# A long convolution on one core: products written over their spectrum, and a last sum of 32x32 tiles in place of transposes

## The chip, the core and the metric

The kernel runs on one core of a Trainium2 chip. The metric is the device time of one launch in microseconds, the median of several runs of the same program. The core has five engines with a queue of instructions each: PE (the 128x128 matrix unit, whose weight loads are listed apart as PEld), DVE (vector), ACT (scalar, activation functions), POOL (general purpose) and SP (which here only issues DMAs). An instruction that waits holds up all that stand behind it in the queue of its engine. Matmuls write to PSUM, four buffers of 128x1024 f32 named p in this stage; DVE or ACT carry a result from there to SBUF, which is called an evacuation below.

## The reference

Two kinds of layer alternate, twice each, over 2048 tokens of 512 channels. Layer A is a gated long convolution along the tokens, layer B an MLP of width 1376. The long convolution is given as an FFT of length 4096:

```python
def _A_ref(q, k, v, shift_k, ssm_k, ssm_D):
    ...
    for t in range(ks):                       # 4 taps along the tokens
        k_shift = k_shift + k_pad[:, t:t + S, :] * shift_k[:, ks - 1 - t][None, None, :]
    kv = k_shift * v
    ...
    y_f = kv_f * kf_f[None, :, :, :]          # spectra of kv and of the filter ssm_k
    y = irfft2(y_f) ...[:, 0, :S, :]
    y = y + kv * ssm_D[None, None, :]
    return q * y

def _B_ref(x, w1, b1, w2, b2):
    y = _layernorm(x, axis=-1)
    h = _gelu(jnp.einsum("bsd,df->bsf", y, w1) + b1)
    return jnp.einsum("bsf,fd->bsd", h, w2) + b2

x = A_q
x = x + _A_ref(_layernorm(x), A_k, A_v, A_shift_k, A_ssm_k, A_ssm_D)
x = x + _B_ref(_layernorm(x), B_w1, B_b1, B_w2, B_b2)
x = x + _A_ref(_layernorm(x), ...)
x = x + _B_ref(_layernorm(x), ...)
```

The convolved y does not depend on x, so it is the same in both layers A. Only the gate, layer norm of x times y, differs.

## The kernel before, in words

The kernel has a planned stage, in which y is computed once and the MLP's first pieces begin, and a dense loop behind it, in which PE runs the MLP's two matmuls back to back (mm1 at L735 with gelu on ACT, mm2 at L769), 4 blocks of 512 tokens in each of the two layers.

The planned stage splits the 512 channels into four chunks of 128 (cc = 0 to 3) and the transform of 2048 tokens into 32 by 64 points. Each step is a piece of work with a name, and a second piece with an e behind its name evacuates it:

- kT and kv (L439, L521): the short convolution of k on PE as matmuls with diagonal weights, for chunks 0 to 2; kvm multiplies by v (L527, DVE). Chunk 3 is done on POOL by kg0 to kg3, ka1 to ka3 (L453, L455, L460) and kgm, which multiplies by v (L464).
- U{cc}S{q}: first stage of the forward transform (L303). U{cc}T{j}: its 32-point pieces are transposed, on PE for chunks 0 to 2 (L335), by two DMA transposes for chunk 3 (L282); the result is ZX.
- kd, KS, K2 (L382, L390, L403): the spectrum of the filter, ZK. K2 are matmuls of 64 rows, two at a time in two groups of rows. The spectrum is needed a second time with the two halves of each complex pair exchanged between partitions; that is KSW, 64 KB further, made by eight copies of 512 KB from SBUF to SBUF by DMA, sa0 to sa3 and sb0 to sb3.
- X{cc}{j}: second stage of the forward transform, eight matmuls of 128 columns into a buffer xb (L551). T{cc}{j}: product with the filter, xb times ZK and KSW in one DVE instruction of 128x2048 into a buffer T (L566). V{cc}{j}: the first step of the inverse, sixteen matmuls whose weights are slices of T against a table Mt of 2 MB that holds the twiddle factors (L575).
- Z, TC, TD and so on: V's results are transposed again, by DMA (L622) or PE (L610). Y: the last step, matmuls of 512 columns with the table GPt (L642). Then for the first block of tokens the gate g (L669, L670), statistics h, p, b (L237, L249, L254), LT (L650, transposing the normed x for the MLP) and M (L698), the first mm1 with its gelu (L706). lx and ly are loads of q, 512 KB and 1536 KB, into x_t.

The order of the work is written out by hand in a string, ORDER. Each of its words names a piece, its engine (P, A, D, G for POOL, S for SP) and its buffers; `_Plan.write` issues the pieces word for word, so each engine's queue has its pieces in the order of the words. The semaphores are put in behind that, by what reads and writes the same range of memory: most of the data lies in one SBUF tile called arena, and the names above are places in it. The product reads both spectra with one access:

```python
kk = at(64 * K + 2 * (ka * D + c0), [[-32 * K, 2], [D, n], [1, CW]])     # KSW, and 64 KB below it ZK
...
eng.tensor_tensor(view(Tb[it["slot"]["T"]], [2, n, CW]), x2, kk, ALU.mult)
```

Of the kernel before, what the change touches and what calls it, by code (L numbers as in the profile page):

```python
# [18 lines left out]
lSK.S wm2.P2 bS.P2 wm0.P1 bSe.A dg0.D dg1.A dg2.A lk0.S lk1.S lh1.S kT0.P2 bSK.P1 bSKe.A kT0e.D kT1.P0 kT2.P3 lh113.S lb1.S lx0.S kT1e.D kT2e.A kT3.P1 wm1.P0 bB.P2 bBe.A lv0.S s00.A lv1.S kT3e.D kv10.P3 kvm10.D kv00.P1 U1S0.P30 kv01.P2 kvm00.D U1S1.P1 U0S0.P01 U1S0e.D lK01.S kg0.G kv11.P3 lK00.S kg1.G U0S0e.A kvm01.D U0S1.P0 s01.G U0S1e.A U0S3.P2 U1S1e.D kvm11.D U0S3e.A kv20.P1 kd0.P0 lK11.S lK10.S kvm20.D kd0e.A U1S3.P3 U0S2.P2 U1S3e.A U0S2e.D KS11.P0 KS11e.A KS01.P1 KS30.P3 KS01e.A lW.S KS00.P2 KS00e.A KS30e.D KS10.P0 KS31.P1 KS10e.D kv21.P3 kvm21.D KS31e.A kd4.P1 kd4e.A KS20.P0 KS21.P2 KS20e.A KS70.P1 KS21e.D KS51.P3 KS41.P0 KS70e.A KS51e.A KS60.P2 KS60e.A KS41e.D KS40.P1 KS61.P3 KS40e.D lX.S KS71.P0 KS50.P2 U1S2.P1 KS71e.D KS61e.A KS50e.A U1S2e.A U2S0.P32 U2S0e.D K25.P0 K25e.A K27.P2 K24.P1 K24e.A K23.P3 K21.P0 K21e.A K27e.D K26.P2 U2S1.P1 K26e.A K23e.D U2S1e.D K20.P3 K28.P0 K20e.A K22.P2 K22e.A K212.P1 K28e.D K215.P3 K215e.A lM.S K212e.D sa1.S sb1.S sa0.S K214.P0 K29.P2 K29e.A K213.P1 U0T0.P3 K214e.D K213e.A K210.P0 K210e.A sb0.S K211.P2 U0T1.P1 s02.D K211e.A U2S3.P0 U0T0e.D U2S3e.A U0T1e.D ka1.G kg2.G ka2.G kg3.G X00.P30 ka3.G kgm.G U3S0.P21 U3S0e.D U2S2.P1 X00e.A X01.P01 lH.S U2S2e.A U1T0.P3 U3S1.P2 T00.D0 U3S3.P1 X01e.A U1T1.P0 sb3.S U1T0e.D X10.P30 U3S1e.A U3S3e.A sa3.S X02.P22 T01.D1 X10e.A U2T0.P1 sb2.S U1T1e.D T10.D2 U3S2.P3 U2T0e.D X02e.A sa2.S X12.P01 V00.P2 U3S2e.A T02.D0 V10.P30 X12e.A X03.P10 V00e.A X03e.A V01.P0 V01e.A X20.P22 T12.D2 X20e.A U3T0.S V12.P1 X11.P01 X11e.A V10e.D lx.S V02.P3 U2T1.P2 T03.D1 X13.P00 T20.D2 V12e.A V02e.A T11.D0 V03.P1 U2T1e.D X13e.A V03e.A X30.P32 T13.D1 V11.P0 X30e.A V11e.D X23.P21 V13.P1 X23e.A U3T1.S V13e.A T30.D0 X22.P30 X22e.A T23.D1 V20.P01 X21.P22 ly.S X21e.A V20e.A V30.P12 X32.P31 T22.D2 T21.D0 X31.P20 V22.P0 X32e.A V21.P3 X31e.A V30e.D X33.P12 V22e.A Z01.S Z00.S X33e.A V23.P2 T32.D2 V23e.A T31.D0 V32.P0 V31.P1 T33b.D1 V33b.P2 T33a.D2 V31e.D Z11.S Z10.S V21e.A V32e.A V33a.P3 Z03.S V33ae.A TC0a.P0 TC0b.P1 Z13.S TC0ae.A TC0be.A w4.S V33be.D TD0b.P3 TD0a.P0 TD0ae.D TC3.P2 TD0be.A Y00.P0 Y01.P3 Y00e.A Y01e.A TC3e.D g00.D w1.S Z02.S TC1.P1 TC1e.A g01.D h00.D Y02.P2 Y32.P0 TC2.P3 Y02e.A h01.D Y32e.A Y10.P1 Y10e.A p00.G w3.S b00.D g02.D p01.G LT0.P2 LT0e.A Y12.P0 Y12e.A M0b.P1 M0be.A TC2e.A h02.D M0a.P2 b01.D LT1.P1 Y30.P0 LT1e.A p02.G b02.D LT2.P3 LG1.D LT2e.D M1a.P1 M0ae.A M1ae.A M1b.P2 M1be.A M2a.P3 M2ae.A M2b.P1 M2be.A M2c.P2 M2ce.A Y30e.A Z12.S w2.S Y20.P3 Y22.P1 Y20e.A Y22e.A  # L19
# [10 lines left out]
def _make_tables():  # L30
# [5 lines left out]
    G = np.zeros((128, 2, 128))  # L36
    for x in range(2):
        for bh in range(2):
            rows = 4 * a + 2 * bh + x
            F[rows, x, bh * 64:bh * 64 + 32] = np.cos(psi)  # L40
            F[rows, x, bh * 64 + 32:bh * 64 + 64] = np.sin(psi)
            for i, p in enumerate(rows):
                G[bh * 64:bh * 64 + 32, x, p] = np.cos(psi[i]) / 64
                G[bh * 64 + 32:bh * 64 + 64, x, p] = np.sin(psi[i]) / 64
# [3 lines left out]
    M = np.zeros((128, NA, 2, 128))  # L48
    for k in range(NA):
        phi = 2 * np.pi * (((k + 0.25) * b / 2048)[:, None] + np.outer(b, k2) / NB)  # L50
        c, s = np.cos(phi), np.sin(phi)
        for bh in range(2):
            cb, sb = c[bh * 32:bh * 32 + 32], s[bh * 32:bh * 32 + 32]
            r, i = bh * 64, bh * 64 + 32
            W[r:r + 32, k, 0:64] = cb
            W[r:r + 32, k, 64:128] = sb
            W[i:i + 32, k, 0:64] = -sb
            W[i:i + 32, k, 64:128] = cb
            for q, sign in ((0, 1.0), (64, -1.0)):
                M[q:q + 64, k, 0, r:r + 32] = sign * cb.T / 32  # L60
                M[q:q + 64, k, 0, i:i + 32] = -sign * sb.T / 32
                M[q:q + 64, k, 1, r:r + 32] = sb.T / 32
                M[q:q + 64, k, 1, i:i + 32] = cb.T / 32
# [5 lines left out]
    q = p % 32  # L69
    M = M[ri][:, :, :, p - q + 16 * (q // 4 % 2) + 4 * (q // 8) + q % 4]  # L70
    GP = G[32 * (p % 4) + p // 4]
# [3 lines left out]
    return tuple(_to_bf16_uint16(t) for t in (F, GP, W, np.roll(W, 64, axis=0), M))  # L75
# [29 lines left out]
def kernel(ctx: ExitStack, tc: tile.TileContext, A_q, A_k, A_v, A_shift_k, A_ssm_k, A_ssm_D,  # L105
                 B_x, B_w1, B_b1, B_w2, B_b2, out):
    nc = tc.nc
# [11 lines left out]
    NZT, NTB = 3, 3  # L119
# [5 lines left out]
    F_np, GP_np, W_np, X_np, M_np = _make_tables()  # L125
    F_h = nc.inline_tensor(F_np, name="tabF")
    GP_h = nc.inline_tensor(GP_np, name="tabGP")
    W_h = nc.inline_tensor(W_np, name="tabW")
    X_h = nc.inline_tensor(X_np, name="tabX")
    M_h = nc.inline_tensor(M_np, name="tabM")  # L130
# [20 lines left out]
    ZK = place("ZK", [P, NA, D], 0)  # L151
    ZX = place("ZX", [P, 2, NA, D // 2], 32 * K)
    Kd = place("Kd", [P, P, NB], 64 * K)
    Wx = place("Wx", [P, NA, P], 88 * K)
    Zk = place("Zk", [P, NA * 2, D // 2], 32 * K)
# [17 lines left out]
    GPt = const.tile([P, 2, P], BF16, name="GPt")  # L173
# [23 lines left out]
    def chunk(t, c):  # L197

        return t[:, c // 2, :, c % 2 * CW:c % 2 * CW + CW]


    ZTb = [big.tile([P, 8 * D], BF16, name=f"ZT{i}") for i in range(NZT)]
    xbb = [big.tile([P, 1024], BF16, name=f"xb{i}") for i in range(3)]
    Tb = [big.tile([P, 2048], BF16, name=f"T{i}") for i in range(NTB)]
# [15 lines left out]
    ZM = "XXPP"  # L220
# [629 lines left out]
```

## Time and profile before

| | us |
|---|---|
| median of 3 runs (lowest, highest) | 249.31 (249.17, 249.37) |
| profiled execution | 249.34 |
| its span, first to last instruction | 247.6 |
| planned stage, to the first mm2 (L769) | 101.4 |
| dense loop behind it | 146.2 |

The profile is one execution of the program. Its times are from the start of the span, and what lies outside the span (1.7 us) is launch and end. A row of a group gives line, engine, operation and tiles, then the count, the busy time in all and the mean in nanoseconds of one. Matmuls are pipelined, so the mean of one is longer than the distance from one to the next; in the chain of waits, which follows the work that ended last back to what released it, a row of matmuls gives their distance. In the timeline a row gives start and duration; an SP row gives the time in which the DMA was being issued, while the landing is in the list of DMA issues.

### The profile page before, as it was taken

The page shows a single profiled execution, that of the slowest core. Times are in us where ns is not written, and L with a number is a line of the kernel's source. Part 1 is how long each engine was busy: PE and PEld are TensorE (multiplying, and loading weights), DVE is VectorE, ACT ScalarE, POOL GpSimd, SP SyncE. Part 2 cuts the span into 40 slices and gives each one's busy share as a digit, 9 for nine tenths or more (in the row PEclk, how much of TensorE's full clock was granted, in tenths as well). Part 3 has the DMA queues.
Part 4 walks back from the last instruction along what each step waited for, and adds up shares of the span by engine and source line. Part 5 has one row for each costly group of instructions (what it writes and reads, how often), then busy time and mean ns, then how long its engine had stood idle before and what let it go on. Part 6 is the DMA issues. An engine that isn't in the chain of part 4 may idle for free.

```text
span 247.6 us, 4783 instructions
## 1 busy us (share of the span) xinstructions
PE 236.1 (95%) x1918; PEld 146.4 (59%) x1929; DVE 171.9 (69%) x315; ACT 145.1 (59%) x218; POOL 54.5 (22%) x50
## 2 busy tenths in 40 slices
PE   4999999899999999999999999999999999999994
PEld 2689877699998688444444444444444444444443
DVE  1467899999997988878889898956956961021022
ACT  5596899899999899707406506505605604704800
POOL 2789999400000221111101111011011010000000
PEclk9999999999999999999999999999999999999998
DMA  6999994946999990040601204013016016011011
GB/s 244 351 292 173 264 437 192 394 175 120 218 254 179 282 260 5 0 85 1 87 0 38 47 3 85 0 23 63 3 44 127 0 45 127 1 42 42 3 42 42
DMA packets 50816, 29.65 MB, mean 120 GB/s; under 512 B 44675, under 2 KB 48488, under 8 KB 49258
## 3 DMA queue, kind: packets, MB, share of 16 engines
q1 hardware_dynamic: 50642, 29.21, 45.7%
q8 instruction: 15, 0.25, 0.4%
q10 hardware_dynamic: 152, 0.14, 0.2%
q14 instruction: 7, 0.06, 0.1%
HBM read 16.23 MB, written 2.10 MB: 74 GB/s over the span
## 4 chain that ended last, share of the span: by engine, by line
PE 72%; DVE 9%; ACT 9%; DMA 5%; issue 2%; POOL 0%; ACTq 0%; DVEq 0%; POOLq 0%
PE po L769 31%; PE ph L735 27%; ACT arena L215 3%; DMA arena<-in_A_v_dram 3%; ACT xb L215 3%; PE p L521 3%; DVE arena L217 3%; ACT ZT L215 2%; DMA arena<-in_A_ssm_D_dram 2%; PE p L698 2%; PE p L303 2%; DVE arena L254 2%; PE p L403 1%; PE p L335 1%; PE p L575 1%
## 5 line engine op out<-in xcount | busy, mean ns | idle before, releaser
L737 ACT ACTIVATE arena<-ph,B 128x512 bf16<-128x512 f32 (+1 forms) x77 | 52.9, 687 | 78.6 <-PE ph L735 78.6
L769 PE MATMUL po<-arena 128*128 128x512 bf16 (+2 forms) x356 | 77.1, 372 | 0.4
L735 PE MATMUL ph<-arena 128*128 128x512 bf16 (+1 forms) x308 | 67.6, 379 | 0.0
L769 PEld LDWEIGHTS <-arena 128*128 128x128 bf16 (+1 forms) x363 | 35.4, 98 | 40.7
L774 DVE TENSOR_TENSOR arena<-po,arena 128x512 bf16<-128x512 f32 (+1 forms) x33 | 21.6, 672 | 44.6 <-PE po L769 44.5
L735 PEld LDWEIGHTS <-arena 128*128 128x128 bf16 (+1 forms) x308 | 30.8, 100 | 35.9
L215 ACT ACTIVATE arena<-p 128x1024 bf16<-128x1024 f32 (+7 forms) x44 | 40.6, 1005 | 3.6 <-PE p L383 1.2
L249 POOL TENSOR_TENSOR lrsm<-lrsm,mhalf 128x4 f32<-128x4 f32 (+2 forms) x10 | 9.1, 910 | 92.3 <-DVE lrsm L243 89.5
L237 DVE BATCH_NORM_STATS2 lstm<-arena 128x6 f32<-128x512 bf16 x32 | 20.0, 681 | 0.2
L215 ACT ACTIVATE ZT<-p 128x1024 bf16<-128x1024 f32 (+1 forms) x18 | 17.9, 1040 | 1.9 <-PE p L303 1.7
L566 DVE TENSOR_TENSOR T<-xb,arena 128x2048 bf16<-128x2048 bf16 (+1 forms) x17 | 18.9, 1153 | 0.0
L254 DVE TENSOR_SCALAR arena<-arena,lmvg,lrsg 128x512 bf16<-128x512 bf16 x32 | 12.9, 465 | 7.3 <-POOL lrsg L249 7.3
L249 POOL TENSOR_TENSOR lrsg<-lrsg,mhalf 128x4 f32<-128x4 f32 x8 | 8.1, 1012 | 44.6 <-DVE lrsg L246 44.6
L237 DVE BATCH_NORM_STATS2 lstg<-arena 128x6 f32<-128x512 bf16 x28 | 17.2, 677 | 0.0
L575 PE MATMUL p<-arena,T 128*128 128x128 bf16 x256 | 16.2, 219 | 0.6 <-ACT ZT L215 0.3
L215 ACT ACTIVATE xb<-p 128x1024 bf16<-128x1024 f32 x16 | 16.3, 1059 | 0.6 <-PE p L551 0.6
L217 DVE COPY arena<-p 128x2048 bf16<-128x2048 bf16 (+3 forms) x12 | 12.3, 1031 | 5.1 <-PE p L439 3.3
L575 PEld LDWEIGHTS <-T 128*128 128x128 bf16 x256 | 14.8, 98 | 1.1 <-issue 0.7
L453 POOL TENSOR_TENSOR T<-arena,SK 128x2048 bf16<-128x2048 bf16 (+3 forms) x4 | 15.0, 3760 | 1.3 <-ACT SK L215 1.1
L254 DVE TENSOR_SCALAR arena<-arena,lmvm,lrsm 128x512 bf16<-128x512 bf16 x32 | 11.5, 416 | 2.8 <-POOL lrsm L249 2.8
L217 DVE CAST arena<-p 128x1024 bf16<-128x1024 f32 x11 | 12.9, 1217 | 0.3
L217 DVE CAST ZT<-p 128x1024 bf16<-128x1024 f32 (+1 forms) x11 | 12.8, 1170 | 0.4 <-ACT arena L215 0.2
(80 smaller groups left out, 249.5 us busy)
## 6 DMA issues: line engine op xcount, KB each, us to landing
arena<-arena SPq DMA_DIRECT2D x8, 512.0 KB, 5.6
arena<-in_A_k_dram SPq DMA_DIRECT2D x2, 1024.0 KB, 6.2
arena<-in_A_v_dram SPq DMA_DIRECT2D x2, 1024.0 KB
arena<-in_A_ssm_k_dram SPq DMA_DIRECT2D x4, 512.0 KB, 12.1
arena<-tabM SPq DMA_DIRECT2D x1, 2048.0 KB
out_dram<-arena SPq DMA_DIRECT2D x15, 128.0 KB, 1.7
arena<-in_A_q_dram SPq DMA_DIRECT2D x1, 1536.0 KB, 6.8
arena<-in_B_w_dram SPq DMA_DIRECT2D x1, 1376.0 KB, 6.7
```

The source lines that it names most:

```text
L215: nc.scalar.activation(dst, src, AF.Copy)
L217: nc.vector.tensor_copy(dst, src)
L237: nc.vector.bn_stats(self.st[:, i, 0, :], x_t[:, GT * g + i, :] if src is None else src[:, i, :])
L249: nc.gpsimd.tensor_tensor(self.rs[:, a:b], self.rs[:, a:b], mhalf[:, a:b], ALU.pow)
L254: nc.vector.tensor_scalar(out=dst[:, i, :], in0=xs, scalar1=self.mv[:, i, 0:1], scalar2=self.rs[:, i:i + 1], op0=ALU.subtract, op1=ALU.mult)
L453: nc.gpsimd.tensor_tensor(m[:, t:NT, :], kn[:, 0:NT - t, c3], sk(t, NT - t), ALU.mult)
L566: eng.tensor_tensor(view(Tb[it["slot"]["T"]], [2, n, CW]), x2, kk, ALU.mult)
L575: nc.tensor.matmul(o[:, i, :], T[:, r, i, :], Mt[:, ka + i, 1 - r, :], start=r == 0, stop=r == 1)
L735: nc.tensor.matmul(o.rearrange("p (i t) -> p i t", t=P), W1t[:, ct, ft * P:ft * P + m], lt[:, a:b, ct, :], start=ct == 0, stop=ct == CT - 1)
L737: nc.scalar.activation(hT[0:m, ft, a * P:b * P], o, AF.Gelu_apprx_tanh, bias=B1[0:m, ft:ft + 1])
L769: nc.tensor.matmul(po[:, a:b], hT[0:m, ft, i * P:(i + 1) * P], W2t[0:m, ft, a:b], start=ft == 0, stop=ft == FT - 1)
L774: nc.vector.tensor_tensor(xs, po[:, a:b], xs, ALU.add)
```

## The change

- The filter's spectrum is made in two halves, chunks 1 and 3 first, then 0 and 2. K2 has 256 matmuls of 128 columns in place of 128 of 256. The eight copies sX are now one pair for each chunk (they were one pair for each quarter of the frequencies), and each waits for all K2 of its half.
- T writes its product over what it has read: over ZK and KSW themselves, with the same access of two steps 64 KB apart. The T buffers are gone; xb has five buffers in place of three.
- V is sixteen matmuls whose weights are slices of that product with a stride of 64 bytes, against a small table Vt. The twiddle factors are no longer in it.
- The transposes Z, TC, TD and their evacuations go (8 DMA transposes and 64 on PE), and the table Mt (2 MB) with them.
- Y is a sum over tiles of 32x32: 512 matmuls of 32 rows, 32 outputs and 128 columns, with the twiddles in the table Yt (1 MB, loaded by lG). Its evacuations write with a stride, and the gate of a unit of one token block reads two halves from PSUM. V's evacuations write Zb, which has two parts of 16 KB, one on each side of x_t.
- Tokens are permuted in the loads of q and the stores of the output, as the last sum gives them in another order. Places in the arena are moved (W1t and W2t, YA, and Zb among them), the sums of POOL's short convolution lie in Yt until it is loaded, and s02 (the layer norm of the first block, L254) comes behind the last product.
- ORDER is written anew.

```diff
-                            nc.tensor.matmul(o[:, par, i, :], (Wt if r == par else Wx)[rs, 2 * j + i, :], Zk[rs, 4 * j + 2 * i + r, :],
...
+                                nc.tensor.matmul(o[:, 4 * par:4 * par + 4, i, :], (Wt if r == par else Wx)[rs, 4 * j + i, :],
+                                                 Zk[hf][rs, 2 * (4 * j + i) + r, :].rearrange("p (f c) -> p f c", f=4),
...
-            KX.append([load(f"s{w}{j}", KSW[a::2, r, :], ZK[1 - a::2, r, :], 1.15 * 2 ** 19, KW[4 * j:4 * j + 4] + (KWp if j == 3 else []))
...
+            for cc in (hf, 2 + hf):
+                r = slice(4 * cc, 4 * cc + 4)
+                KX[cc] = [load(f"s{w}{cc}", KSW[a::2, r], ZK[1 - a::2, r], 1.15 * 2 ** 19, KW[hf] + KWp[hf])
...
-                        eng.tensor_tensor(view(Tb[it["slot"]["T"]], [2, n, CW]), x2, kk, ALU.mult)
...
-                                nc.tensor.matmul(o[:, i, :], T[:, r, i, :], Mt[:, ka + i, 1 - r, :], start=r == 0, stop=r == 1)
...
-        lM = load("lM", Mt[:], M_h.ap().bitcast(BF16), 2 ** 21, kvp)
...
+        lG = load("lG", Yt[:], Y_h.ap().bitcast(BF16), 2 ** 20, [kgm])
...
+                    kk = at(64 * K + 2 * (c0 * NA + k0 * 32), [[-32 * K, 2], [32 * NA, 4], [1, 256]])
...
+                    (nc.vector if it["eng"] == "D" else nc.gpsimd).tensor_tensor(kk, x2, kk, ALU.mult)
...
+                            nc.tensor.matmul(o[:, i, :], at(64 * K * w + 2 * (c0 * NA + m0 + i), [[32, P]]), Vt[:, w, :],
+                                             start=w == 0, stop=w == 1)
...
+                                 lambda cc=cc, m0=m0: Zb[:, :, :, 32 * cc + m0:32 * cc + m0 + 8],
...
-                            nc.tensor.transpose(o[:, x, t, c * P:(c + 1) * P], zsrc(cc, 8 * g + GT * x + t0 + t, [[32, P]]), IDt[:])
...
-                        nc.tensor.matmul(o[:, i, :], GPt[:, x, :], V2[g][:, x, t0 + i, :], start=x == 0, stop=x == 1)
...
+                                    rs, b = slice(64 * hh + 32 * jj, 64 * hh + 32 * jj + 32), 16 * bh + GT * g + t0 + t
+                                    nc.tensor.matmul(o[32 * bh:32 * bh + 32, jj, t, :], Yv[rs, b, r, :], Zb[rs, r, b, :],
+                                                     start=r == 0, stop=r == 1)
...
+kg2.G sa3.S sb1.S sa1.S K200e.A ... ka2.G kg3.G ka3.G kgm.G X10e.A U3S0.P01 ... T11.D T13.D sb3.S U0T0e.D ... T10.D sb0.S U2T0e.D ... sa0.S T00.D ... sa2.S sb2.S T02.D
```

Three queues show how copies and products stand to each other. In the rows, `arena<-arena 64x4096` on SP is one of the copies sX; DMAHW0 to DMAHW7 are eight counters of landed DMAs, of which each new DMA takes the next (the first copy takes DMAHW2 in both programs). A wait on an engine's name is one on a certain instruction of that engine.

SP before, from the table Mt on. The copies are sa1, sb1, sa0, sb0, then (behind GPt) sb3, sa3, sb2, sa2; behind them U3T0 and lx:

```order
L279 DMA arena<-tabM 128x8192 [waits DVE_49,PE_49,DMAHW1_49,Activation_49,Pool_49]
L279 DMA arena<-arena 64x4096 [waits DMAHW5_49,DMAHW6_49,DMAHW2_49,Activation_49]
L279 DMA arena<-arena 64x4096 [waits DMAHW3_49]
L279 DMA arena<-arena 64x4096 [waits DMAHW4_49,DVE_49,Activation_49]
L279 DMA arena<-arena 64x4096
L279 DMA GPt<-tabGP 128x256
L279 DMA arena<-arena 64x4096 [waits DMAHW0_49,DVE_49,DMAHW7_49,PE_49,Activation_49]
L279 DMA arena<-arena 64x4096
L279 DMA arena<-arena 64x4096 [waits DMAHW1_49,Activation_49]
L279 DMA arena<-arena 64x4096 [waits DMAHW2_49,Pool_49]
L282 DMA_TRANSPOSE arena<-ZT_94 128x16x128 [waits DMAHW3_49,DVE_49,Activation_49]
L279 DMA arena<-in_A_q_dram 128x2048 [waits DMAHW4_49,PE_49,Pool_49]
```

There the waits on DVE and ACT are for evacuations of K2. SP now, the same place: sa3, then sb1 and sa1, then sb3, the table Yt, sb0, sa0, sa2, sb2, U3T0, lx, U3T1 and ly:

```order
L270 DMA arena<-arena 64x4096 [waits DMAHW4_49,DMAHW3_49,DMAHW5_49,DMAHW2_49,DMAHW6_49,DVE_49,DMAHW7_49,PE_49,Pool_49]
L270 DMA arena<-arena 64x4096 x2
L270 DMA arena<-arena 64x4096 [waits DVE_49,Pool_49]
L270 DMA Yt<-tabY 128x4096
L270 DMA arena<-arena 64x4096 [waits DVE_49,Activation_49]
L270 DMA arena<-arena 64x4096 [waits DMAHW0_49,DVE_49]
L270 DMA arena<-arena 64x4096 [waits DMAHW1_49,DVE_49]
L270 DMA arena<-arena 64x4096 [waits DMAHW2_49]
L273 DMA_TRANSPOSE arena<-ZT_95 128x16x128 [waits DMAHW3_49,DMAHW4_49,DMAHW2_49,DMAHW5_49,DMAHW1_49,DMAHW7_49,DMAHW0_49,Activation_49]
L270 DMA arena<-in_A_q_dram 128x1x2048 [waits Activation_49]
L273 DMA_TRANSPOSE arena<-ZT_95 128x16x128
L270 DMA arena<-in_A_q_dram 128x1x6144 [waits DMAHW6_49,PE_49]
```

The instructions behind the names are: sa3's PE is the last matmul of K2; sb3's DVE is the product T13 and its Pool is kgm; sb0's DVE is the product T10; sa0's DVE is the evacuation U2T0e; sa2's DVE is the product T00; lx's Activation is the evacuation of V13. So five of eight copies and a load of q moved behind products or what follows from products.

DVE before, where the products begin (`T<-xb,arena` is a product, `arena<-p 128x16x128` the evacuation of a transpose U{cc}T{j}):

```order
L217 CAST ZT_94<-p_119 128x256x4 [waits PE_49,Activation_49]
L566 TENSOR_TENSOR T_99<-xb_96,arena 128x2048 [waits DMAHW4_49,DMAHW3_49,DMAHW5_49,Activation_49,Pool_49]
L217 COPY arena<-p_120 128x16x128 [waits PE_49]
L566 TENSOR_TENSOR T_100<-xb_97,arena 128x2048 [waits DMAHW3_49,DMAHW6_49,DMAHW2_49,Activation_49]
L217 COPY arena<-p_117 128x16x128 [waits PE_49]
L566 TENSOR_TENSOR T_101<-xb_96,arena 128x2048 [waits Activation_49]
```

DVE now, at the same place: T11, T13, U0T0e, U0T1e, T12, T10, U2T0e, T00, T02:

```order
L554 TENSOR_TENSOR arena<-xb_97,arena 128x2x4x256 [waits DMAHW3_49,DMAHW4_49,DMAHW2_49,Activation_49]
L554 TENSOR_TENSOR arena<-xb_98,arena 128x2x4x256 [waits DVE_49]
L209 COPY arena<-p_120 128x2048 [waits DMAHW5_49,PE_49,Activation_49]
L209 COPY arena<-p_117 128x2048 [waits PE_49,Activation_49]
L554 TENSOR_TENSOR arena<-xb_100,arena 128x2x4x256 [waits Activation_49]
L554 TENSOR_TENSOR arena<-xb_99,arena 128x2x4x256
L209 COPY arena<-p_118 128x2048 [waits DMAHW7_49,PE_49,Activation_49]
L554 TENSOR_TENSOR arena<-xb_98,arena 128x2x4x256 [waits DMAHW6_49,DMAHW0_49,Activation_49]
L554 TENSOR_TENSOR arena<-xb_97,arena 128x2x4x256 [waits DMAHW2_49,DMAHW1_49,PE_49]
```

The counters DMAHW2, 3 and 4 of the first row are the landings of sa3, sb1 and sa1; DMAHW5 is sb3, DMAHW7 sb0, DMAHW0 sa0, and DMAHW2 and 1 of the last row are sb2 and sa2. An evacuation U0T0e or U2T0e, which had waited for PE alone, now waits for a copy.

POOL before, the last three instructions of the short convolution of chunk 3 and what is ahead of them (kg3, ka3, kgm):

```order
L460 TENSOR_TENSOR T_99<-T_99,T_101 128x2048 [waits Pool_49]
L453 TENSOR_TENSOR T_101<-arena,SK 128x1664 [waits Pool_49]
L455 TENSOR_TENSOR T_101<-kh,SK 128x384
L460 TENSOR_TENSOR T_99<-T_99,T_101 128x2048 [waits Pool_49]
L464 TENSOR_TENSOR arena<-arena,T_99 128x16x128 [waits DMAHW2_49,DMAHW1_49,Pool_49]
```

and POOL now:

```order
L456 TENSOR_TENSOR Yt<-Yt 128x2048 [waits Pool_49]
L449 TENSOR_TENSOR Yt<-arena,SK 128x1664 [waits DMAHW3_49,DMAHW4_49,DMAHW2_49,Pool_49]
L451 TENSOR_TENSOR Yt<-kh,SK 128x384
L456 TENSOR_TENSOR Yt<-Yt 128x2048 [waits Pool_49]
L460 TENSOR_TENSOR arena<-arena,Yt 128x16x128 [waits DMAHW1_49,Pool_49]
```

In kg3 stands a wait for three landings, which are again sa3, sb1 and sa1; before, it had none. U3S0 on PE, the first stage of the transform for chunk 3, reads what kgm writes. Further on, the product T32 needs an evacuation on ACT that stands behind V03's evacuation, and that one waits for the landings of lx and ly; T33, the last product, stands behind T32, and seven of the sixteen V stand behind T33 on PE.

304 lines of the change are left out of this document (125 added, 179 removed).

## The prediction

> **What bounds the kernel now.** I read the page's busy times and its 40 slices first, to see whether one engine bounds the whole, then the table by windows, to see the limit of each stage, then the chain of waits.
>
> ```profile
> span 247.6 us, 4783 instructions
> ...
> PE 236.1 (95%) x1918; PEld 146.4 (59%) x1929; DVE 171.9 (69%) x315; ACT 145.1 (59%) x218; POOL 54.5 (22%) x50
> ...
> PE   4999999899999999999999999999999999999994
> ...
> PEclk9999999999999999999999999999999999999998
> ...
> 50.00:60.00 10.00, 9.93 (x161) 9.63 (x159) 10.00 (x10) 9.94 (x11) 0.00 (x0) 1.00 0.43 127
> 60.00:70.00 10.00, 9.80 (x173) 9.58 (x171) 10.00 (x10) 10.00 (x12) 0.00 (x0) 1.00 1.09 240
> ...
> 101.37:247.60 146.23, 142.25 (x664) 66.06 (x669) 88.41 (x211) 55.26 (x80) 13.10 (x13) 0.99 0.19 40
> ```
>
> Behind each window stand its length and the busy time of PE, PEld, DVE, ACT and POOL. From 50 to 70 us PE, DVE and ACT are all full: nobody waits long, and a delay on one engine has nothing to hide in. From 101.37 on PE is dense (142 of 146 us), and the diff leaves that stage's matmuls alone. So the question is when the dense stage can start. The chain of waits shows what leads there:
>
> ```profile
> 30.96 3.56 ACT arena L215 x4
> ...
> 35.70 3.05 PE p L403 x48
> ...
> 51.48 0.87 PE p L303 x8
> 52.35 1.01 PE p L335 x16
> 53.36 0.89 PE p L551 x16
> ...
> 75.20 3.24 ACT ZT L215 x4
> 78.44 0.28 ACT arena L215
> 78.73 0.02 issue
> 78.75 1.73 PE p L610 x24
> ...
> 99.91 1.46 PE p L642 x6
> 101.37 9.51 PE po L769 x44
> ```
>
> It hops in pieces of one to four microseconds between PE and the two evacuating engines, without one large wait. Two moments matter: the last evacuation of a V product ends at 78.7, and the dense stage starts 22.7 us behind it, at 101.4.
>
> **The change part by part.** The filter copies come first, because the order printed above ties them to the products. Today's queues:
>
> ```profile
> 40.25 3.62 SPq L279 DMA_DIRECT2D arena<-arena  x4
> 43.92 1.21 SPq L279 DMA_DIRECT2D GPt<-tabGP  x1
> 45.74 3.21 SPq L279 DMA_DIRECT2D arena<-arena  x4
> ...
> 58.93 0.93 SPq L279 DMA_DIRECT2D arena<-in_A_q_dram  x1
> 59.92 4.82 SPq L282 DMA_TRANSPOSE arena<-ZT  x1
> 64.83 0.53 SPq L279 DMA_DIRECT2D arena<-in_A_q_dram  x1
> ...
> 33.41 3.39 POOL L453 TENSOR_TENSOR T<-arena,SK 128x1664 bf16<-128x1664 bf16 x1
> ...
> 41.90 4.09 POOL L464 TENSOR_TENSOR arena<-arena,T 128x2048 bf16<-128x2048 bf16 x1
> ...
> 50.59 1.22 DVE L566 TENSOR_TENSOR T<-xb,arena 128x2048 bf16<-128x2048 bf16 x1
> 51.72 1.22 DVE L217 COPY arena<-p 128x2048 bf16<-128x2048 bf16 x1
> ...
> arena<-arena SPq DMA_DIRECT2D x8, 512.0 KB, 5.6
> ...
> out_dram<-arena SPq DMA_DIRECT2D x15, 128.0 KB, 1.7
> arena<-in_A_q_dram SPq DMA_DIRECT2D x1, 1536.0 KB, 6.8
> ...
> 40.00:50.00 10.00, 8.80 (x125) 7.17 (x122) 9.93 (x11) 8.81 (x10) 5.92 (x2) 1.00 0.86 344
> ...
> L403 PE MATMUL p<-arena x64: 267/269/280, 35.7 to 45.4; 64*128 64x256 bf16 x64
> ```
>
> All eight copies are issued by 49, POOL's last four instructions (from 33.41 to 45.99, 12.6 us, kgm the last of them) wait for no copy, and the first product starts at 50.59: copies and POOL are hidden. In the changed program a product reads and writes one access that steps from the filter to its copy 64 KB away, and the program orders copies and products against each other. Following SP, POOL, DVE and PE in the order, each wait with the instruction that satisfies it, I get a serial walk. Its prices: copies take their bytes at the 344 GB/s of that window and the 1.7 us of the smallest lone transfer (out_dram): one 3.2 us, two 4.8, three 6.3. The bounds of a lone copy are 1.7 (latency alone) and 5.6 (today's median, four in a row); 3.2 is taken since nothing else is queued then. A product, or a spectrum's evacuation on DVE, repeats every 1.13 us (50.59 to 51.72). An evacuation on ACT takes 0.9 (four in 3.56). Sixteen matmuls of V take 1.0, as L335's, whose weights are strided like V's new ones.
>
> - The last K2 starts at 45.4 now. Ahead of it PE gets two U1T (1.01 each), U2S3 and X11 (half of 0.87 and of 0.89), and loses U0T0 (1.01): +1.9. Twice as many K2 matmuls of half the columns are the same columns; I cost them at nothing (at most 2 us, if each has a floor of its own). The loads ahead are reordered too, but PE is at 9 in those slices, so its pieces set that end: 47.3.
> - sa3 waits for that K2, whose weights Wx it overwrites; sb1 and sa1 are queued behind it on SP. All landed: 53.6.
> - kg3 on POOL waits for those three (today for none), then 12.6 us to kgm's end: 66.2. U3S0 on PE waits for kgm, and behind it in PE's queue stand all further transposes and X: PE idles from about 49 to 66.
> - sb3 waits for kgm, and DVE's queue behind T13 for sb3. It shares the engines with the 1 MB table Yt, so it is priced halfway between one and three copies, 4.7: 70.9. Four DVE pieces (U0T0e, U0T1e, T12, T10): 75.4.
> - sb0 waits for T10, U2T0e for sb0 (3.2 + 1.1: 79.7); sa0 for U2T0e, T00 for sa0 (3.2 + 1.1: 84.0); sa2 and sb2 for T00, T02 for them (4.8: 88.8).
> - T02, T03, T01 (3.4) and V11, V12, V13 (3.0), which wait for each other, then V13's evacuation (0.9): 96.1.
> - lx waits for that evacuation; ly is queued behind lx and a DMA transpose. Today it is 5.9 us from lx to ly (58.93 to 64.83) and 6.8 to land: 108.8. V03's evacuation on ACT waits for both, since its strided destination spans x_t; three more stand behind it (3.6 in all): 112.4. T32 needs the last of them.
> - T32, V01, X33, V23, T33 in turn (4.7), seven V that stand behind T33 (7.1), one evacuation (0.9): 125.1. Today that point is 78.7.
>
> The tail is today's 22.7 us and a difference. The 64 transposes of L610 go (1.73 us for 24, 72 ns each): -4.6. The 32 old Y matmuls go (1.46 for 6, 243 ns): -7.8. The new Y is 512 matmuls of 32x32 tiles by 128 columns, and no row shows such tiles. A full one of 128 columns takes 56 ns (L551, 0.89 for 16): one by one that is 28.7 us, with all eight tiles of a set side by side 3.6. The nearest row is L403, whose two groups of 64 rows take 64 ns for 256 columns (3.05 for 48) where full matmuls take 109 (L303, 0.87 for 8), so nearly two at a time. I take two at a time, 28 ns: 14.3. The difference is +1.9 and the tail 24.6: the dense stage starts at 149.7.
>
> Costed at nothing: the eight DMA transposes of Z and the smaller tables, since their queues are not what the walk waits for; the evacuations of the removed transposes (about 1 us each, ACT and DVE), whose place the evacuations of the Y halves take; s02, four of L254 on DVE, which moves behind the last product and is covered by the seven V. Uncovered it would be 2.9 us:
>
> ```profile
> 44.01 2.88 DVE arena L254 x4
> 4.14 3.31 PE L420 MATMUL p<-Ft 128*128 128x512 bf16 x8
> ```
>
> **Sum:** 149.7 - 101.4 = +48.3 us. The profiled execution took 249.34 us for its span of 247.6, and the median of the runs is 249.31, so they agree. 249.3 + 48.3 = 297.6; I say 298. Ends: with lone copies at 1.7 (-3.0), sb3 at 3.2 (-1.5), lx to ly without the transpose's 4.82, and Y at 3.6 (-10.7) it is 278; with lone copies at 5.6 (+4.8), sb3 at 6.3 (+1.6), K2's floor (+2), s02 uncovered (+2.9) and Y at 28.7 (+14.4) it is 323. Not all go one way: 281 to 318.
>
> [...] The last row above is PE's start: eight matmuls of 512 columns at 414 ns, where the chain's 44 at 101.37 take 216. Behind that the clock's slices read 9 in all but the last, so this trace has no PE that has idled for 17 us. [...]
>
> **The rivals.**
> - *The waits don't bite* (the other side). If copies have landed and products ended before the waiting word is reached, the added 46 us of the middle vanish and Y decides: 249.3 - 4.6 - 7.8 + Y, and 0.12 us for each of 16 V with strided weights (1.01 against 0.89). With Y at 3.6 that is 242; it is faster as long as Y is under 10.5 us (20 ns a matmul), and at 14.3 it is 253. For it: today all copies are hidden. Against it: kg3, the head of 12.6 us, can't start before three copies that themselves wait for the last K2, and sb3 waits for kgm. Chance 0.06, 0.04 of it faster.
> - *Fewer hops.* Single waits are met early: lx and ly (12.7), if DMA reaches them sooner than I reckon, or the copies' latency is the low bound. 298 - 12.7 - 4.5 = 281, with a quick Y 270. Chance 0.15.
> - *A cold PE.* With PE at half speed behind its waits, the 12 V on the walk take 1.0 more each and Y 14.3 more: 324. For it: idle stretches of many us. Against: within the walk PE is used every few us. Chance 0.09.
> - *Y one by one:* 28.7 in place of 14.3, 312, inside the range. Chance 0.10.
> - *The change doesn't do what it says* is excluded: no queue has Z's DMA transposes or L610's any more.
>
> [...]
>
> **How the numbers follow.** The walk as summed has 0.60, and the rivals above the rest. A difference of 0.2% (0.5 us) is about what a measurement of this kernel can tell from no change. Faster by more than that is only the first rival with a quick Y: 0.04; within it 0.01; slower 0.95. The range of 278 to 320 holds the walk, Y one by one and the part of "fewer hops" with a slow Y; outside lie the first rival, the cold PE and the quick part of "fewer hops", 2 in 10 together.
>
> **What would show it.** Right: PE's slices have gaps between 49 and 110 us; kg3 on POOL starts near 53 in place of 33.4; sb3, sb0, sa0 and sa2 stand apart on SP between 66 and 89, with DVE waiting for each; ACT waits for a load of q near 109; the first matmul of the dense stage starts near 150, and from there it takes its 146 us. Wrong: kg3 runs near 34; DVE's products run back to back from 50; Y takes 4 us or 28.

## The result, and the profile after

The changed kernel takes 340.57 us (median of 4 runs, 339.64 to 341.62) where the kernel before takes 249.31: the ratio is 1.366 (95% interval 1.362 to 1.370). The forecast was 298, with a range of 278 to 320. The direction was right and the amount was not: +91 us instead of +49. The profiled execution took 341.62 us for a span of 339.8.

The page of the changed kernel, the rows that answer to those shown of before:

```profile
span 339.8 us, 5841 instructions
...
PE 247.4 (73%) x2473; PEld 158.4 (47%) x2473; DVE 178.9 (53%) x332; ACT 135.2 (40%) x201; POOL 55.8 (16%) x48
...
PE   3779999006429330005869999999999999999994
...
PEclk9959999656957855555978999999999999999999
```

PE's busy time grew little (247.4 against 236.1 us), but its slices now have a hole at 60 to 76 us, a patchy stretch, and a second hole at 127 to 153. In both the granted clock falls, to 0.50 in the two windows below.

The table by windows, with the same columns as before (length, PE, PEld, DVE, ACT, POOL, clock, DMA share, GB/s):

```profile
66.00:78.00 12.00, 0.00 (x0) 0.00 (x0) 3.61 (x1) 0.00 (x0) 11.84 (x4) 0.50 0.00 0
126.00:150.00 24.00, 0.00 (x0) 0.00 (x0) 0.99 (x1) 0.00 (x0) 0.00 (x0) 0.50 0.43 84
...
192.36:339.80 147.44, 142.73 (x672) 66.09 (x671) 87.71 (x205) 54.56 (x82) 13.10 (x13) 1.00 0.18 40
```

From 66 to 78 us POOL is nearly alone. From 126 to 150 no engine does anything to speak of, and the DMA engines move 84 GB/s. The dense stage takes 147.4 us (146.2 before) and starts at 192.36 instead of 101.37: 91.0 of the 92.2 us by which the span grew lie ahead of it. The chain of waits names what stands there:

```profile
5.26 14.02 DMA arena<-in_B_b_dram
...
59.14 4.83 DMA arena<-arena
...
64.13 4.40 POOL Yt L449
...
78.67 5.29 DMA arena<-arena
...
88.78 2.82 DMA arena<-arena
...
92.98 2.85 DMA arena<-arena
...
97.68 3.58 DMA arena<-arena
...
102.67 1.92 PE p L562 x16
...
110.39 0.63 SPq L270
...
111.07 8.77 SPq L273
...
119.95 31.00 DMA arena<-in_A_q_dram
...
161.88 7.28 PE p L562 x111
```

The serial walk of the prediction is there, step by step and in its order: three copies, kg3 on POOL, sb3, sb0, sa0, sa2 with sb2, then V, lx, a DMA transpose and ly. One step in it is 31 us long where 6.8 was forecast, and the walk starts 10 us late.

### The profile page after: what moved, and what is told of

It reads as the page before. It is cut to its first block, busy times and chain, and to the rows that moved or that the text cites. A ratio compares the mean times of both kernels' runs of the same rounds, so it can differ in the third digit from the quotient of the medians.

```text
span 339.8 us, 5841 instructions
## 1 busy us (share of the span) xinstructions
PE 247.4 (73%) x2473; PEld 158.4 (47%) x2473; DVE 178.9 (53%) x332; ACT 135.2 (40%) x201; POOL 55.8 (16%) x48
## 4 chain that ended last, share of the span: by engine, by line
PE 57%; DMA 20%; DVE 8%; POOL 4%; ACT 4%; SPq 3%; issue 2%; DVEq 0%; POOLq 0%; ACTq 0%
PE po L715 22%; PE ph L681 20%; DMA arena<-in_A_q_dram 9%; DMA arena<-arena 6%; DMA arena<-in_B_b_dram 4%; DVE arena L209 4%; PE p L516 4%; PE p L562 4%; SPq L273 3%; PE p L644 2%; DVE arena L554 2%; ACT arena L207 2%; DMA Ft<-tabF 1%; POOL Yt L449 1%; POOL arena L460 1%
## 5 line engine op out<-in xcount | busy, mean ns | idle before, releaser
L207 ACT ACTIVATE arena<-p 128x1024 bf16<-128x1024 f32 (+6 forms) x57 | 44.3, 831 | 59.0 <-DMA arena<-in_A_q_dram 36.9
L562 PE MATMUL p<-Vt,arena 128*128 128x128 bf16 x256 | 21.9, 254 | 47.3 <-ACT arena L207 27.5
L554 DVE TENSOR_TENSOR arena<-xb,arena 128x2048 bf16<-128x2048 bf16 x16 | 22.3, 1419 | 56.2 <-ACT xb L207 27.8
L562 PEld LDWEIGHTS <-arena 128*128 128x128 bf16 x256 | 20.2, 155 | 48.6 <-DVE arena L554 48.6
L207 ACT ACTIVATE ZT<-p 128x1024 bf16<-128x1024 f32 x13 | 13.3, 1027 | 33.0 <-PE p L294 33.0
L294 PE MATMUL p<-Ft,arena 128*128 128x256 bf16 x64 | 10.0, 291 | 18.8 <-POOL arena L460 18.6
L209 DVE CAST arena<-p 128x1024 bf16<-128x1024 f32 (+1 forms) x20 | 20.0, 1032 | 6.3 <-PE p L562 3.9
L209 DVE COPY arena<-p 128x2048 bf16<-128x2048 bf16 (+3 forms) x10 | 10.3, 1036 | 21.8 <-DMA arena<-arena 17.5
L228 DVE BATCH_NORM_STATS2 lstg<-arena 128x6 f32<-128x512 bf16 x32 | 19.7, 680 | 3.7 <-DMA arena<-in_A_q_dram 3.7
L449 POOL TENSOR_TENSOR Yt<-arena,SK 128x2048 bf16<-128x2048 bf16 (+3 forms) x4 | 15.9, 3997 | 33.7 <-DMA arena<-arena 29.3
L542 PE MATMUL p<-arena,Wt 128*128 128x128 bf16 x128 | 10.5, 236 | 7.4 <-DMA arena<-ZT 5.3
L294 PEld LDWEIGHTS <-arena 128*128 128x128 bf16 x64 | 6.1, 104 | 20.0 <-POOL arena L460 18.8
```

The lines of the kernel that those rows point to most:

```text
L207: nc.scalar.activation(dst, src, AF.Copy)
L209: nc.vector.tensor_copy(dst, src)
L228: nc.vector.bn_stats(self.st[:, i, 0, :], x_t[:, GT * g + i, :] if src is None else src[:, i, :])
L294: nc.tensor.matmul(o[:, i, :], src[:, 4 * q + i, cs], Ft[:, 0:256], start=True, stop=True)
L449: nc.gpsimd.tensor_tensor(m[:, t:NT, :], kn[:, 0:NT - t, c3], sk(t, NT - t), ALU.mult)
L554: (nc.vector if it["eng"] == "D" else nc.gpsimd).tensor_tensor(kk, x2, kk, ALU.mult)
```

## The experiments

All but the last experiment were run once. The changed kernel's own four runs spread over 2.0 us and the last experiment's four over 3.5, so a difference of less than about 3 us between single runs decides nothing, and there the trace is read instead.

**The loads of q.** The changed kernel loads q with its tokens permuted. The source of each of its three loads has an outermost dimension of 4 (`rows`: [NT*D, 4], then [4*NT*D, 32], then the tokens), with 32 partitions behind each. In this kernel each of the three, lx0, lx and ly, is four loads of 32 partitions; the diff shows lx0:

```diff
-lx0 = load("lx0", at4(145 * K, GT), rows(q_d, 0, GT), 2 ** 19)
+def loadq(name, off, t0, t1, nbytes, deps=()):
+    def fn(it):
+        for a in range(4):
+            nc.sync.dma_start(at(off, [[1, (t1 - t0) * D]], 32 * a, 32),
+                              apf(q_d, (a * NT + t0) * D, [[4 * NT * D, 32], [1, (t1 - t0) * D]]))
+    return plan.add(name, {"S": 400}, deps, fn, dma=("copy", nbytes))
+lx0 = loadq("lx0", 145 * K, 0, GT, 2 ** 19)
```

> The changed kernel with its three loads of q (lx0, lx, ly) each written as four DMAs of 32 partitions in place of one DMA whose source has an outer dimension of 4; bytes and places are the same. Theory A (the permuted load runs on 4 of the 16 DMA engines): ly lands about 7 us after its issue in place of 31, lx to ly takes about 6 us in place of 9.6, and the loads ahead of the filter are no longer held up, so that the last K2 ends near 48 in place of 57.7: together 340.6 - 24 - 3.6 - 10 = 303 us. Theory B (ly is slow because it competes with the weight loads queued behind it, and the early stage is late because of its new order): ly still takes 25 us or more, K2 ends at 57, the time stays at 335 or more.

It took 311.8 us, 28.8 less (303 had been expected: the last K2 came 3.2 us earlier and not 10). Its chain, at the place of the 31 us:

```profile
107.82 1.98 SPq L273
...
111.88 8.47 DMA arena<-in_A_q_dram
```

The same bytes land 8.5 us after the last of the four issues, and the DMA transpose ahead of them on SP takes 1.98 us instead of 8.77. The reverse, on the kernel before, again shown for lx0 and done for all three:

```diff
+def rows(d, t0, t1):
+    return apf(d, t0 * D, [[NT * D, 4], [4 * NT * D, P // 4], [1, (t1 - t0) * D]])
...
-lx0 = load("lx0", lna0, xd[:, 0:GT, :], 2 ** 19)
+lx0 = load("lx0", at(145 * K, [[1, GT * D]]), rows(q_d, 0, GT), 2 ** 19)
```

> The kernel before with nothing changed but its three loads of q, written with the changed kernel's access (outer dimension 4); the output is then that of permuted tokens against an unpermuted convolution, so it is another sum, with the same work. Theory A (4 of 16 DMA engines): lx0 holds up the loads of the early stage by some 8 us, ly lands 30 us after its issue and not 7, at about 100 with the delay, which the first layer norm statistics of the second block wait for: 260 to 270 us. Theory B (the loads alone do nothing): 249 to 251 us.

It took 279.07 us where the kernel before took 249.3 beside it: +29.8 from the form of three loads alone. Of that, 8.9 us are there at the first K2 (44.57 against 35.70), and 20.65 are one wait of PE further on. SyncE's queue of this kernel, and the window in which PE waits:

```profile
67.68 8.24 SPq L285 DMA_TRANSPOSE arena<-ZT  x1
76.01 0.60 SPq L282 DMA_DIRECT2D arena<-in_A_q_dram  x1
76.70 27.44 SPq L625 DMA_TRANSPOSE arena<-arena  x2
```

```profile
84.17:104.82 20.65, 0.00 (x0) 0.00 (x0) 0.40 (x1) 1.82 (x2) 0.00 (x0) 0.60 0.28 66
```

With little else in flight, 0.28 of the sixteen DMA engines' time is busy, at 66 GB/s: 4.5 engines' worth. (In the changed kernel's hole it is 0.43, where weights issued behind ly are under way as well.) Here the transposes of Z are queued behind ly: they hold SyncE until 104.14, and PE, for which the profile names no releaser, goes on at 104.82. In the changed kernel it is V03's evacuation that waits. Theory A of the two expectations above (4 of the 16 engines) is near these 4.5, and the 31.0 us of ly against the 8.5 us of the four loads of 32, 3.7 times as long, go with it. Which engines carried the packets, and what sets their number, no trace shows.

**What ties the copies to kg3.** The prediction held the product's access, which steps from the filter to its copy 64 KB away, responsible. Two experiments, each from the changed kernel. One splits the product:

```diff
-kk = at(64 * K + 2 * (c0 * NA + k0 * 32), [[-32 * K, 2], [32 * NA, 4], [1, 256]])
...
-x2 = apf(xb, xb.offset, [list(xb.ap[0]), [0, 2], [256, 4], [1, 256]])
-(nc.vector if it["eng"] == "D" else nc.gpsimd).tensor_tensor(kk, x2, kk, ALU.mult)
+for half in (64 * K, 0):
+    kk = at(half + 2 * (c0 * NA + k0 * 32), [[32 * NA, 4], [1, 256]])
+    (nc.vector if it["eng"] == "D" else nc.gpsimd).tensor_tensor(kk, xb, kk, ALU.mult)
```

> The changed kernel with each product T as two DVE instructions, one over ZK and one over KSW, so that no access spans both. If the product's wide access is what ties copies and products (the prediction's reason), the hops sb3, sb0, sa0, sa2 go: about 340.6 - 13 - 5 = 322 us or less. If it is the copies that are described too widely, the hops stay, since evacuations of transposes hold the same copies up: 337 to 343 us, with some 1 to 2 us more of DVE.

329.1 us: 11.5 less, between the two expectations. kg3 still starts at 63.8 us, behind 29.1 us of waiting for copies; what went is part of the hops behind it. The other describes the same bytes of a copy by one flat access in place of a slice of a four-dimensional view:

```diff
-r = slice(4 * cc, 4 * cc + 4)
-KX[cc] = [load(f"s{w}{cc}", KSW[a::2, r], ZK[1 - a::2, r], 1.15 * 2 ** 19, KW[hf] + KWp[hf])
+def half(k0, a, cc):
+    return apf(arena, a * ROW + (k0 * K + 8 * K * cc) // 2, [[2 * ROW, P // 2], [1, 4 * K]])
...
+KX[cc] = [load(f"s{w}{cc}", half(64, a, cc), half(0, 1 - a, cc), 1.15 * 2 ** 19, KW[hf] + KWp[hf])
```

> The changed kernel with the same eight copies, each described as 64 partitions of one run of 4096 elements in place of a slice of a four-dimensional view; the bytes are the same. If the description of the copies is what makes them conflict with everything in the arena, kg3 on POOL runs at 35 in place of 64, PE's idle 17 us behind the last K2 go, and the lone copies follow each other at once: 340.6 - 15 - 15 = 310 us, with the wait for ly left as it is. If the product's access is the cause, the time stays at 335 or more.

320.46 us: 20.1 less, where 30 had been expected. POOL's timeline has kg3 nearly where it is in the kernel before, with no wait, and 1.0 us shorter than in the changed kernel:

```profile
34.72 3.39 POOL L450 TENSOR_TENSOR Yt<-arena,SK 128x1664 bf16<-128x1664 bf16 x1
```

So kg3's wait came from how the copies are written, not from how the products are: described as a four-dimensional slice, the copies are ordered against work on bytes that they don't touch. ly still takes its 30.39 us here. Both repairs together:

> Both mends in one kernel: q loaded by 32 partitions (311.8 us alone) and the copies described as flat runs (320.5 alone). If the two causes are separate, their gains add: 340.6 - 28.8 - 20.1 = 291.7, within 3 us. If they are the same time twice over (a copy late only because loads held up the engines before it), 300 or more.

292.2 us. 28.8 and 20.1 separately, 48.4 together: the causes add, and between them they carry more than half of the 91.

**What stands behind.** From here each kernel builds on the one ahead of it. First, the destination of V's evacuations in one piece, so that it no longer spans x_t, with lx, U3T1 and ly issued as soon as U3T0 is:

```diff
-Zb = at(96 * K, [[16 * K, 2], [P, NB], [1, P]])
+Zb = at(96 * K, [[8 * K, 2], [P, NB], [1, P]])
...
-x_t = place("x_t", [P, NT, D], 112 * K)
+x_t = place("x_t", [P, NT, D], 128 * K)
...
-... U3T0.S ... T20.D lx.S ... V02.P2 U3T1.S ... X31e.A ly.S V03e.A
+... U3T0.S lx.S U3T1.S ly.S V11.P1 ... T20.D ... V02.P2 ... X31e.A V03e.A
```

> As loads_and_flat, and Zb lies in one piece of 32 KB with x_t behind it (before: one half of Zb on each side of x_t), and lx, U3T1 and ly stand right behind U3T0 on SP. If V03's evacuation waits for lx and ly only because its strided range spans x_t, that wait goes: some 13 us less than loads_and_flat, 277 to 281. If another wait stands right behind it, less than 5 us.

287.02 us: only 5.2 less; what the place of Zb and the place of the loads give apart was not run. The chain shows the wait that took its place:

```profile
82.81 4.23 DMA arena<-in_A_q_dram
...
87.08 1.22 DVE arena L561
```

Now a product waits for q, whose bytes it doesn't touch. Next, all copies are issued as soon as their K2 evacuations are done:

```diff
+K213e.A sa1.S sb1.S U1T0.P0 ... sa3.S K200e.A sb3.S sb0.S sa0.S sa2.S sb2.S U2S2.P3
-K213e.A U1T0.P0 ... sa3.S sb1.S sa1.S K200e.A U2S2.P3 ... T13.D sb3.S ... T10.D sb0.S ... X01.P04 sa0.S ... V10.P3 sa2.S sb2.S
```

> As zb_in_one_piece, with sa1 and sb1 right behind the last evacuation of their half of the filter and the other five copies right behind sa3. If the rest of the loss in the middle stage is copies that stand behind products in the order, the products run nearly back to back from the last K2 (54) on: V done some 30 us later as in the kernel before, dense stage from about 108: 255 to 262 us. If the two-step access of a product still ties it to copies of other chunks, 265 or more.

276.92 us: 10.1 less. The products' wait stays, and is now the only large one:

```profile
76.33 8.05 DMA arena<-in_A_q_dram
...
84.44 1.23 DVE arena L561
```

Then the product in two, as above, on top of it:

> As copies_at_once, with each product as two DVE instructions. If the two-step access still ties products to copies of other chunks, this gains over copies_at_once by more than the 1.6 us that the 16 extra instructions cost; if not, it is slower by 1 to 2 us.

262.87 us: 14.1 less, though each product now costs two instructions. The products start at 56.4 us, and DVE waits for no copy and no load of q from there on. So the prediction's knot, the access that steps over 64 KB, exists too; it ties products to q's loads and to V's matmuls (in the kernel ahead DVE's products waited 14.4 us for V and V 8.9 us for products, here neither shows), and it became visible once the copies' own knot was gone. How it ties them is not shown: the access lies below 96 KB and q's place begins at 128 KB, so its span alone doesn't reach q. Whether the sign of its step (-64 KB) matters was not run.

**The start.** The first step of the filter's transform (kvm on DVE) begins at 19.64 us in that kernel, at 24.62 in the changed one and at 14.53 before. On DVE, s00 (the statistics of q's first tokens) stands ahead of it; ACT has it in the kernel before. DVE and POOL of the last kernel:

```profile
13.43 2.46 DVE L228 BATCH_NORM_STATS2 lstg<-arena 128x6 f32<-128x512 bf16 x4
15.80 0.36 DVE L232 BATCH_NORM_AGGREGATE lmvg<-lstg 128x2 f32<-128x6 f32 x4
16.20 3.53 DVE L237 TENSOR_SCALAR lrsg<-lmvg 128x4 f32<-128x4 f32 x1
19.64 2.34 DVE L529 TENSOR_TENSOR arena<-p,arena 128x1024 bf16<-128x1024 f32 x2
```

```profile
11.77 7.93 POOL L450 TENSOR_TENSOR Yt<-arena,SK 128x2048 bf16<-128x2048 bf16 x2 [3.85 <-DVE SK L209]
```

DVE's L237, an instruction of four elements a partition, takes 3.53 us and ends, at 19.73, when POOL's pair of products ends (19.70). s00 back on ACT (`s00.D` becomes `s00.A`):

> As copies_at_once_product_in_two (262.9 us), with the statistics of the first block, s00, on ACT as in the kernel before. In copies_at_once_product_in_two DVE spends 13.43 to 19.73 on them with the first kvm queued behind, while ACT is idle. If that is the rest of the early stage's delay, the first kvm comes near 14.6 in place of 19.64, K2 ends 4 to 5 us earlier, and the time is 258 to 259. If the loads or POOL's chain set the early stage, less than 1.5 us.

264.09 us, no gain: kvm starts at 17.83, but PE then waits until 22.14 for ACT, which has the evacuation of the small matrix B queued behind s00. With sa0 and sb0 issued first and sa3 and sb3 last (`sa0 sb0 sa2 sb2 sa3 sb3`):

> As stats_on_act, with the six late copies in the order sa0, sb0, sa2, sb2, sa3, sb3, in which the products need them. If each product waits only for its own chunk's copies, 2 to 4 us less than stats_on_act; if the first V waits for all eight (its strided weights), no change within 1 us.

262.62 us, not to be told apart from the last two. The first V starts at 65.30, against 65.96 with the other order, though the last K2 is 1.7 us earlier here, so the order brought nothing. In the kernel with the product in two, ahead of these, the chain has it behind a copy:

```profile
58.54 6.75 DMA arena<-arena
...
65.75 3.16 PE p L569 x32
```

That V belongs to chunk 1, whose own two copies were issued first, from 48.37 on; the copy it waits for is the last of the eight. That V's strided weights wait for all eight copies fits this. So one kernel keeps sa1, sb1, sa0 and sb0 in front, and issues sa2, sb2, sa3 and sb3 only behind V13:

> As stats_on_act, with sa2, sb2, sa3 and sb3 behind V13 in the order. If the first V waits for every copy that is ahead of it in the order, it now starts some 5 us earlier (four copies in flight and not eight), 253 to 256 us; if it waits for its own chunk's two copies anyway, there is no gain, or a loss of the 5 us that the late copies then cost.

273.0 us, some 9 to 10 slower: the first V starts 4.5 us earlier than with s00 on ACT alone (61.5), 2.5 of which are there at the last K2 already, but an evacuation waits for the late copies, which go behind q's load and land in 11.27 us:

```profile
71.80 11.27 DMA arena<-arena
...
83.18 1.03 ACT arena L207
```

Last, s00 on DVE again but behind kvm20, otherwise as with sa0 and sb0 first, run four times:

```diff
-lb1.S s00.A kg0.G ... kvm20.D U1S0e.A
+lb1.S kg0.G ... kvm20.D s00.D U1S0e.A
```

> As stats_on_act_sa0_first (262.6 us), with s00 back on DVE but behind kvm20 in the order. In stats_on_act the first kvm came early (17.83), and PE then waited until 22.1 for the evacuation of the bias, which ACT had behind s00. If that in-order wait is what took the gain back, the first kvm now comes near 16 and PE goes on at once, K2 ends 3 to 5 us earlier than 54, and the time is 258 to 260. If the early stage hangs on the loads or on PE's own work, 262 or more.

261.27 us (260.23 to 263.76), 1.051 of the kernel before (95% interval 1.044 to 1.057). In it the same four-element instruction runs while POOL has no product under way:

```profile
24.86 0.17 DVE L237 TENSOR_SCALAR lrsg<-lmvg 128x4 f32<-128x4 f32 x1
```

kvm now starts at 15.86 instead of 19.64, but the last K2 at 51.8 instead of 53.9. Part of the head start is lost to s00 itself: the chain goes through it from 22.17 to 24.90, and the next kvm starts behind it.

**The account.** One after another, the repairs take away:

| Cause | us |
|---|---|
| q's loads with an outermost dimension of 4 | 28.8 |
| copies described as four-dimensional slices | 19.6 |
| Zb spanning x_t, place of lx and ly | 5.2 |
| copies issued behind products | 10.1 |
| product stepping over 64 KB | 14.1 |
| s00 and the order of the copies | 1.6 (within the spread) |
| left to the kernel before | 11.9 |

The shares of the middle depend on this order (the product in two is worth 11.5 alone and 14.1 here). No version run is as fast as the kernel before. Of what is left, the last kernel's trace shows this (its profiled span is 10.9 us longer than before's): 2.6 to the first K2, 3.8 within the K2, 2.7 from there to the last V's evacuation (PE waits 3.2 us for copies before the first V), 0.6 in the tail, 1.2 in the dense stage. Its stretch of K2 and then before's, by windows:

```profile
38.30:52.00 13.70, 13.55 (x317) 11.79 (x317) 11.26 (x11) 13.40 (x15) 9.32 (x4) 1.00 0.20 80
```

```profile
35.70:45.70 10.00, 9.92 (x149) 8.00 (x149) 9.67 (x8) 9.54 (x11) 9.84 (x4) 1.00 0.68 282
```

PE is full in both; K2 itself is the same 8.1 us in both (256 matmuls at 32 ns, 128 at 64), and the rest is other work that now stands between its two halves. Whether an order exists that gives this back later was not tried.

## Why the prediction was right and wrong

The walk, with its own steps (end of each, us from the span's start):

| Step | Forecast | Measured | Miss |
|---|---|---|---|
| last K2 (sa3 issued) | 47.3 | 57.7 | +10.4 |
| sa3, sb1, sa1 landed | 53.6 | 64.0 | 0 |
| kg3 to kgm | 66.2 | 78.7 | +2.1 |
| sb3 | 70.9 | 84.0 | +0.6 |
| four DVE pieces; sb0, sa0, sa2 and sb2 | 88.8 | 101.4 | -0.5 |
| T02 to V13's evacuation | 96.1 | 110.4 | +1.7 |
| lx, ly landed | 108.8 | 150.95 | +27.9 |
| four evacuations | 112.4 | 154.8 | +0.3 |
| T32 to T33 | (4.7) | 161.8 | +2.3 |
| seven V and evacuation | 125.1 | 170.2 | +0.4 |
| tail | 149.7 | 192.36 | -2.5 |

**lx and ly: the step that failed.** "5.9 us from lx to ly and 6.8 to land" took an ordinary load's row for a load of another form. The diff shows the form (an outer dimension of 4), and I read it as a permutation of tokens and not as something with a price. Measured: 9.6 to ly's issue and 31.0 to land, so a step of 12.7 us took 40.6. The DMA transpose in between was slowed as well (8.77 us, 1.98 with the loads repaired). Repaired, the whole kernel gained 28.8.

**The last K2.** "The loads ahead are reordered too, but PE is at 9 in those slices, so its pieces set that end" failed. From the first kvm to the last K2 it is 32.8 us against 30.9 before, the +1.9 of the sum; the first kvm itself came 10.1 late. PE waited until 19.33 for a load of 2.7 KB that was 14.02 us on its way behind lx0; DVE's s00 waited for lx0 itself, and kvm stood behind s00. The 2 us that the upper end of the sum has for a floor of each K2 matmul don't show: one of 128 columns takes 31 ns (1.00 us for 32), one of 256 took 64 before (3.05 for 48). With the loads repaired the last K2 ends 3.2 us earlier, in the last experiment, with s00 behind kvm, 5.7. There it starts at 51.8, 4.5 behind the forecast's 47.3: 2.6 of these are there at the first K2, and 1.9 are work between the K2 beyond the +1.9 of the sum. Why the start keeps the 2.6 is not shown.

**kg3, sb3, sb0, sa0, sa2 one after another** was right in order and nearly in size: a lone copy took 2.82 and 2.85 (forecast 3.2), a pair 3.58 behind its last issue and 4.1 in all (4.8), sb3 5.3 (4.7), three 6.3 (6.3). The reason given for it was half of the truth: kg3 was tied by the copies' own description, as the flat copies show; the product's access ties other things. The waits had been read off the built program's queues, so their places came out right though the reason for them was partly mistaken.

**kg3 to kgm** was 1.9 us short on POOL. kg3 took 4.40 us instead of 3.39 and the short piece behind it (L451) 1.86 instead of 0.93. DVE's first products now wait for the same three copies and run beside these two (last section).

**The tail.** The step "two at a time, 28 ns" for the new Y was too dear. Its rows:

```profile
L586 PE MATMUL p<-arena,Yt 32*32 32x128 bf16 x512 | 6.3, 245 | 1.5 <-ACT arena L207 0.9 <-DVE arena L617 0.6
```

```profile
191.70 0.66 PE p L586 x64
```

The last 64 take 10.3 ns each, and all 512 keep PE busy for 6.3 us, against the forecast's 14.3. A full matmul of 128 columns takes 56, the time of 5.4 of these, and the low end of the forecast (3.6 us) was the nearer one. But the tail is only 0.5 us shorter than before, so the table's -2.5 is luck in part: Y is 8.0 us cheaper than forecast, and 5.5 us that the sum didn't have stand against it. The tail of the changed kernel, its two halves, and the tail of the kernel before, by windows:

```profile
170.21:192.36 22.15, 18.84 (x661) 16.72 (x661) 19.88 (x53) 17.04 (x51) 3.41 (x5) 0.85 0.01 4
170.21:181.75 11.54, 8.46 (x420) 7.33 (x420) 10.20 (x29) 6.61 (x18) 2.15 (x4) 0.70 0.02 4
181.75:192.36 10.61, 10.37 (x245) 9.38 (x243) 9.68 (x26) 10.43 (x33) 1.26 (x2) 1.00 0.01 3
```

```profile
78.70:101.37 22.67, 21.78 (x233) 17.10 (x238) 19.52 (x43) 21.30 (x47) 3.58 (x5) 1.00 0.62 163
```

PE does 2.9 us less work, part of it at a lower clock (0.70 in the first half), and waits 2.4 us more. The waits are in the first half, the longest (2.27 us) for DVE's normalisation; DVE, with gate, statistics and normalisation, is busy there for 10.20 of 11.54 us. In the second half PE is full again. This is where the gain that the change does bring went.

**A cold PE** was a rival with a chance of 0.09, its price 26 us. It was there, beside the walk and not in its place: the clock is 0.50 in both holes, sixteen matmuls of V took 1.92 us behind a wait (102.67, clock 0.50) where they take about 1.05 later on (161.88, 7.28 for 111, clock 1.00). Most of the +1.7 and +2.3 of the table fits it, though no run took it away alone. "PE is used every few us" was wrong for the two holes, in which PE ran nothing for 18.6 and 27.5 us. What brings the clock down, and after how long, was not run.

**The other side** (the waits don't bite) would have needed the copies, the products and q's loads repaired together. Even then, the last kernel is at 261 and not at 242 or 253: its K2 ends late, and its tail takes 23.27 us, at a clock of 0.78, against 22.67 before.

## What to carry to other kernels

Price a changed load by its access pattern: the row of 6.8 us was good for a load of its own form, and with an outermost dimension of 4 the same bytes took 31.0. Where a framework works out the waits from how an access is described, describe the same bytes as plainly as possible (for the copies that alone was worth 20.1 us), and repair such knots together, since behind each removed wait the next one stood. A reduction of one engine's work shows in the time only where that engine is what the stretch waits for: 2.9 us less of PE's work made the tail 0.5 us shorter.

## What was not expected of the hardware

DMAs queued behind q's loads in their outer-4 form were slow: behind lx0 a load of 2.7 KB took 14.02 us, and behind lx a DMA transpose took 8.77 us, against 1.98 with q loaded by 32 partitions.

DVE and POOL were slower beside each other in two places. The four-element instruction above took 3.53 us beside POOL's products and 0.17 without them, and in the changed kernel two products took 5.52 us beside kg3, itself at 4.40 instead of 3.39, where two in a row take 2.35 in the kernel with all copies at once. DVE's timeline of the two pairs:

```profile
64.09 5.52 DVE L554 TENSOR_TENSOR arena<-xb,arena 128x2048 bf16<-128x2048 bf16 x2 [4.00 <-DMA arena<-arena]
```

```profile
56.76 2.35 DVE L561 TENSOR_TENSOR arena<-xb,arena 128x2048 bf16<-128x2048 bf16 x2
```

The four-element instruction ends 0.03 us behind POOL's products (19.73 and 19.70). What the two engines wait for in that time no trace shows. Not every pair of instructions does this: in the kernel before, DVE's evacuations run beside kg3 at their usual 1.2 us each, and kg3 takes its 3.39.
